# Reordering the second products of a two-stage mixture-of-experts kernel, with five smaller moves around them

## The chip, the cores and the metric

One NeuronCore of one Trainium2 chip runs the whole program. The metric is device time in microseconds (us) from one launch to its end; a kernel's time is the median of its runs. The names used here: PE is TensorE, DVE is VectorE, ACT is ScalarE, POOL is GpSimd, SP is SyncE, whose only work here is to issue DMAs.

## What is computed

The reference is three layers in a row, all in float32.

```python
def reference(**kwargs):
    attn_out = _attn_ref(q, k, v)                 # 2 x 8 heads, 768 rows, 64 wide, windowed
    x = attn_out as (1536 tokens, 512)
    x = _moe_ref(x, w_gate, w1, w2)               # each token through ONE of 8 experts (argmax)
    return _moe2_ref(x, w_gate, w1, w2)           # every token through ALL 8 experts

def _moe2_ref(x, w_gate, w1, w2):
    logits = x @ w_gate
    P = np.exp(logits - logits.max())
    for _ in range(8):                            # the "mixing"
        P /= P.sum(1, keepdims=True) + 1e-09
        P /= P.sum(0, keepdims=True) + 1e-09
        P *= N / E
    for e in range(E):
        h = np.maximum(x @ w1[e], 0.0)            # 1536 x 512 times 512 x 1024
        out += P[:, e:e + 1] * (h @ w2[e])        # 1536 x 1024 times 1024 x 512
    return out
```

## The kernel before

**First mixture (lines 775 to 1000).** Tokens are sorted by expert into blocks of 256 rows; seven blocks run here. `layer1` makes the hidden rows, `layer2` multiplies them with `w2`: two row groups `s` of 128 rows, eight chunks `fc` of the hidden size, three matmuls for each pair (the values are kept as a high and a low part). Before the change both groups go through `fc` 0 to 3 together, then group 0 through 4 to 7, then group 1. When a group is done its sum of squares is taken (L931), it is scaled (L936) and scattered to rows of `yd` in DRAM by an indirect DMA from POOL's queue (L937). Between the groups the next block's rows are turned on PE (`turn_rows`, L892, L897, L898). `step()` takes the next item of a list of weight loads and splits for the next block. Up to here a planner with a cost model decides each engine's order from when it thinks operands are ready; the program's order only breaks ties.

**Second mixture (lines 1000 to 1500).** Every product of four 2x2 quarters is done with seven products and additions (Strassen-Winograd form), so operands need sums. `tokens(j)` fetches a pair of 128-token tiles from `yd` (one of each half of the tokens), turns them on PE (L1066), copies them out (L1070), and makes the high and low part of seven operands: `part1` to `part5`, with the additions `sums12` and `sums34`. Its `logits` multiplies with the gate and, for each second pair, writes the operands to DRAM.

From L1477 on the order of each engine is written out by hand as a loop over ticks. Each tick issues what `plan` holds for it, then one first product (`first`, six matmuls: one of seven operands `i`, for one of four column chunks `fc`), and on every other tick one second product (`second`, twelve matmuls). An expert `e` takes 84 ticks; s below is its first tick, and the second products run 38 ticks behind. What follows a first product is spread over the next ticks (`operands2`): rounding the three raw parts (L1290, L1293), four additions on DVE (L1296 to L1299), rounding the four sums on ACT and DVE (L1302, L1305). They recur every seven ticks; "phase" below is the tick modulo 7, and the four additions are at phase 0, L1302 at phase 3 ahead of the eviction of first product 3 (called C1 below, L1257), L1305 at phase 4.

**The seven second products** of a group of 128 rows accumulate in two PSUM tiles. `gx` takes products 0, 3, 5, 6 one upon the other, each evicted before the next may be added: x0, x3, x5, x6. `ga` has two halves: y1, and z2 with z4 added to it. Evictions go to `acc`: products 2 and 4 by DVE (L1366), the others by ACT into `y` tiles (L1374), which two accumulating DMAs from POOL add to `acc` (L1368, L1376). For expert 0 nothing is scaled: products 4 and 5 are added by DVE (L1358), the rest are copied by ACT. For the last expert all are evicted by DVE and sent out by SP. After the last first product, second products are issued one per tick.

**Weights and mixing.** A `Piece` is a quarter of an expert's `w1` or `w2`: loaded, squared on ACT (`measure`, L690), its scale found through a PE matmul (`measured` L694 on DVE, then `rate` L699), sums made by POOL (L707, L711), and both parts written (L715 on ACT, L720 on DVE). The last quarter of `w2` takes over a buffer of the expert before, so `second` itself issues its splits at products 4 and 6 of the last row group. `mixing` is the eight rounds of normalising, 12 x 8 values per partition, each round two steps between ticks 66 and 115, where expert 0's second products and expert 1's weight splits run too.

## Time and profile before

| | before |
|---|---|
| median of 3 runs | 1277.93 us (1274.8 to 1278.49) |
| the profiled execution | 1278.5 us, of it a span of 1276.7 us |
| mean granted clock of PE | 0.979 of 2.4 GHz |
| PE busy | 1196.2 us (94%) |
| DVE, ACT, POOL busy | 999.5 (78%), 849.2 (67%), 364.1 us (29%) |
| chain that ended last, by engine | PE 66%, DVE 18%, DMA 7%, issue 5%, ACT 4% |
| attention and sorting | 0 to about 128 us |
| first mixture | about 128 to 320 us |
| second mixture | about 320 us to the end |

The span runs from the first to the last instruction; the rest of an execution's time, 1.8 us here, lies around it. PE's busy time is modelled and covers the overlap of matmuls, so PE's waits and the starts of its products say more than its share. A product's matmuls follow each other faster than the length that a row gives for one of them: 12 of them start within 1.31 us, while one is shown 0.27 us long. A wait is counted from the shown end, so a stall costs PE 0.16 us (0.27 less 1.31/12) more than its wait.

### The profile page before, as it was taken

Reading aid. Unit: us, or ns where it says so; the run is one execution under the profiler, and the core shown is the slowest. Engines: PE = TensorE matmul, PEld = TensorE weight load, DVE = VectorE, ACT = ScalarE, POOL = GpSimd, SP = SyncE. Lnnn points to the kernel's source line nnn. Section 1 sums busy time; section 2 is a strip of 40 time slices with the busy share of each in tenths; the row PEclk is TensorE's granted clock in tenths of the full one; section 3 lists DMA queues with packets and bytes.
Section 4 is the critical chain, followed back from the end, with each engine's and each line's share of the span. In section 5 each row is a group of like instructions: output and inputs, shape, how many; then the busy total and the mean of one; then the engine's idle time right before and its main releaser. Section 6 shows DMA issues by size and latency. Waiting matters only on the chain.

```text
span 1276.7 us, 27622 instructions
## 1 busy us (share of the span) xinstructions
PE 1196.2 (94%) x10551; PEld 1054.5 (83%) x10551; DVE 999.5 (78%) x1823; ACT 849.2 (67%) x1599; POOL 364.1 (29%) x412
## 2 busy tenths in 40 slices
PE   5898999999789889999999999999999999999997
PEld 5776879888578778888888888888888888888886
DVE  6695678975498899887888788788868878886674
ACT  5585578765476757776876776677668767775541
POOL 4351212102013142333434243243413334331000
PEclk8799999999799999999999999999999999999999
DMA  9954888764334414635444564445555534553201
GB/s 199 202 96 146 260 258 267 254 205 155 126 105 137 117 59 127 154 92 136 112 113 127 127 162 104 100 116 133 125 132 142 123 95 122 141 125 79 80 34 50
DMA packets 177597, 173.59 MB, mean 136 GB/s; under 512 B 32864, under 2 KB 149472, under 8 KB 177072
## 3 DMA queue, kind: packets, MB, share of 16 engines
q1 hardware_dynamic: 163888, 143.75, 39.1%
q0 software_dynamic: 13568, 27.99, 11.3%
q8 instruction: 85, 1.39, 0.5%
q14 instruction: 56, 0.46, 0.1%
HBM read 136.10 MB, written 15.53 MB: 119 GB/s over the span
## 4 chain that ended last, share of the span: by engine, by line
PE 66%; DVE 18%; DMA 7%; issue 5%; ACT 4%; SPq 1%; POOL 0%; DVEq 0%; ACTq 0%; POOLq 0%
PE gx L1336 16%; PE fx L1250 15%; PE ga L1336 12%; PE fa L1250 11%; DMA raw<-in_moe_w 3%; PE ph L814 3%; PE py L833 3%; DVE w1l L720 2%; DVE hl L1293 2%; DVE c L1260 1%; DVE wl L781 1%; DVE c L1297 1%; DVE c L1298 1%; DMA xl<-xold 1%; DVE c L1299 1%
## 5 line engine op out<-in xcount | busy, mean ns | idle before, releaser
L1336 PEld LDWEIGHTS <-hh 128*128 128x128 f16 x2688 | 263.2, 98 | 55.0 <-issue 24.4
L1250 PEld LDWEIGHTS <-w1h 128*128 128x128 f16 x2688 | 260.4, 99 | 49.4 <-issue 16.4
L1336 PE MATMUL gx<-w2h,hh 128*128 128x256 f16 x768 | 209.5, 273 | 7.7 <-DVE acc L1358 4.9
L1250 PE MATMUL fx<-xh,w1h 128*128 128x256 f16 x736 | 201.7, 274 | 9.2 <-ACT c L1257 4.8
L1336 PE MATMUL gx<-w2h,hl 128*128 128x256 f16 x768 | 209.5, 273 | 0.0
L1336 PE MATMUL gx<-w2l,hh 128*128 128x256 f16 x768 | 209.5, 273 | 0.0
L1250 PE MATMUL fx<-xl,w1h 128*128 128x256 f16 x736 | 201.6, 274 | 1.7 <-POOL xl L1076 1.0
L1250 PE MATMUL fx<-xh,w1l 128*128 128x256 f16 x736 | 201.8, 274 | 0.0
L1305 DVE TENSOR_TENSOR hl<-c,hh 128x1024 f16<-128x1024 f32 x96 | 120.5, 1255 | 84.1 <-ACT hh L1302 83.9
L707 POOL TENSOR_TENSOR raw<-raw 128x256 f32<-128x256 f32 x168 | 158.8, 960 | 55.9 <-ACT raw L690 46.9
L1336 PE MATMUL ga<-w2h,hh 128*128 128x256 f16 x576 | 157.0, 273 | 14.2 <-DVE acc L1366 14.2
L1257 ACT ACTIVATE c<-fx,kap 128x256 f32<-128x256 f32 x288 | 131.8, 473 | 54.5 <-PE fx L1250 53.0
L1336 PE MATMUL ga<-w2h,hl 128*128 128x256 f16 x576 | 157.1, 273 | 0.0
L1336 PE MATMUL ga<-w2l,hh 128*128 128x256 f16 x576 | 157.0, 273 | 0.0
L1250 PE MATMUL fa<-xh,w1l 128*128 128x256 f16 x552 | 151.6, 275 | 0.0
L1250 PE MATMUL fa<-xh,w1h 128*128 128x256 f16 x552 | 151.6, 275 | 0.0
L1250 PE MATMUL fa<-xl,w1h 128*128 128x256 f16 x552 | 151.6, 275 | 0.0
L1250 PEld LDWEIGHTS <-w1l 128*128 128x128 f16 x1344 | 132.2, 98 | 18.1 <-issue 1.9
L1336 PEld LDWEIGHTS <-hl 128*128 128x128 f16 x1344 | 131.5, 98 | 15.2
L1302 ACT CAST hh<-c 128x1024 f16<-128x1024 f32 x96 | 99.9, 1040 | 51.4 <-DVE c L1299 51.2
L1374 ACT ACTIVATE y<-gx,pws 128x256 f32<-128x256 f32 x144 | 68.1, 473 | 95.3 <-PE gx L1336 82.4
L711 POOL TENSOR_TENSOR raw<-raw 128x256 f32<-128x256 f32 x56 | 58.6, 1047 | 222.5 <-issue 155.1
(261 smaller groups left out, 2629.7 us busy)
## 6 DMA issues: line engine op xcount, KB each, us to landing
raw<-in_moe_w SPq DMA_DIRECT2D x64, 512.0 KB
raw<-in_moe_w SPq DMA_DIRECT2D x228, 128.0 KB
xh<-xohd SPq DMA_DIRECT2D x147, 128.0 KB
xl<-xold SPq DMA_DIRECT2D x147, 128.0 KB
acc<-y POOLq DMA_DIRECT2D x72, 256.0 KB, 4.3
raw<-in_moe_w SPq DMA_DIRECT2D x38, 256.0 KB
vt<-in_v SPq DMA_DIRECT2D x16, 240.0 KB
raw<-yd SPq DMA_DIRECT2D x12, 260.0 KB
```

Source lines behind the costliest of these rows:

```text
L707: eng.tensor_tensor(out=r[to], in0=r[x], in1=r[y], op=ALU.add if sign > 0 else ALU.subtract)
L711: eng.tensor_tensor(out=self.raw[:, 2], in0=self.raw[:, 2], in1=self.raw[:, 5 if self.second else 4], op=ALU.add)
L720: nc.vector.scalar_tensor_tensor(out=lo[:, w], in0=self.raw[:, s], scalar=wsc[self.x][:, self.i : self.i + 1], in1=hi[:, w], op0=ALU.mult, ...
L814: nc.tensor.matmul(ph, a, c[:, kc], start=kc == 0 and m == 0, stop=kc == KC - 1 and m == 2)
L833: nc.tensor.matmul(pys[s], a, c, start=fc == 0 and m == 0, stop=fc == FC - 1 and m == 2)
L1250: nc.tensor.matmul(p, l[:, a, kc * P : (kc + 1) * P], r[:, j, kc], start=new and kc == 0 and m == 0, stop=kc == K2 - 1 and m == 2, skip_gr ...
L1257: nc.scalar.activation(c[:, q], p, f, scale=k_)
L1293: nc.vector.scalar_tensor_tensor(out=h[1][:, :3], in0=raw, scalar=0.0, in1=h[0][:, :3], op0=ALU.max, op1=ALU.subtract)
L1302: nc.scalar.copy(h[0][:, 3:], c)
L1305: nc.vector.tensor_tensor(out=h[1][:, 3:], in0=c, in1=h[0][:, 3:], op=ALU.subtract)
L1336: nc.tensor.matmul(p, l, r, start=new and f == 0 and m == 0, stop=f == F2 - 1 and m == 2, skip_group_check=True)
L1374: nc.scalar.activation(gs["s"][:, d], p, AF.Copy, scale=w)
```

## The change

Six things are done:

1. `layer2`: both row groups go together through `fc` 0 and 1 only; then group 0 through 2 to 7, two steps, group 1 through 2 to 7.
2. The first two token pairs load, turn and split their first halves before their second halves.
3. The gate products of all pairs (`LOGITS`) come one or two ticks later; of expert 1's pieces four `rate` matmuls come two or three ticks later, and three of their squares move by one tick.
4. The mixing's two scalings per round go from DVE to POOL, each round gets a third step, and the constant NT/E moves into the column sum's scaling.
5. The seven second products run in the order x0, y1, x3, z2, x5, z4, x6 (before: x0, y1, z2, x3, z4, x5, x6). Each row half gets a `y` tile of its own. For expert 0, product 5 is copied by ACT into a `y` tile and added to `acc` by a DMA from POOL ("staged"), instead of being added by DVE.
6. The last quarter's splits are put into the plan at ticks of their own, 1 to 7 ticks after product 4, instead of at products 4 and 6. Its buffer is held four ticks longer, by which one other piece of each expert from the third on loads and splits three ticks later.

```diff
@@ layer2 @@
-        half = FC // 2
-        for fc in range(half):
+        for fc in range(2):
             for s in range(ns):
                 product(s, fc)
-            if fc % 2:
+        step()
+        step()
+        for s in range(ns):
+            for fc in range(2, FC):
+                product(s, fc)
+            if s == 0:
                 step()
                 step()
-        for s in range(ns):
-            for fc in range(half, FC):
-                product(s, fc)
             yield s, pys[s]
...
@@ tokens @@
-        def load():
+        def load(halves=(0, 1)):
...
-            for half in range(2):
+            for half in halves:
...
@@ mixing @@
-            nc.vector.tensor_tensor(out=pw, in0=pw, in1=r.unsqueeze(2).to_broadcast(sh), op=ALU.mult)
+            nc.gpsimd.tensor_tensor(out=pw, in0=pw, in1=r.unsqueeze(2).to_broadcast(sh), op=ALU.mult)
+
+        def turn2():
             cs.append(g2.tile([P, E], F32, tag="c", name="c"))
...
-            nc.vector.tensor_scalar(c, pc, 1e-9, None, op0=ALU.add)
+            nc.vector.tensor_scalar(c, pc, 1e-9, float(E / NT), op0=ALU.add, op1=ALU.mult)
             nc.vector.reciprocal(c, c)
-            nc.vector.scalar_tensor_tensor(
-                out=pw, in0=pw, scalar=float(NT / E), in1=c.unsqueeze(1).to_broadcast(sh), op0=ALU.mult, op1=ALU.mult
-            )
+            nc.gpsimd.tensor_tensor(out=pw, in0=pw, in1=c.unsqueeze(1).to_broadcast(sh), op=ALU.mult)
...
@@ second @@
-    SECOND = (
-        (H11, V11, "x", True),
-        (H12, V21, "y", True),
-        (R1, V1, "z", False),
-        (R2, V2, "x", False),
-        (R4, V22, "z", False),
-        (R3, V3, "x", False),
-        (H22, V4, "x", False),
-    )
+    SECOND = {
+        0: (H11, V11, "x", True),
+        1: (H12, V21, "y", True),
+        3: (R2, V2, "x", False),
+        2: (R1, V1, "z", False),
+        5: (R3, V3, "x", False),
+        4: (R4, V22, "z", False),
+        6: (H22, V4, "x", False),
+    }
...
             if i == 4:
-                last[e + 1].raw_hi()
-                last[e + 1].raw_lo()
-                last[e + 1].sum4()
-            elif i == 6:
-                last[e + 1].sum_hi()
-                last[e + 1].sum_lo()
+                p4 = last[e + 1]
+                for d, f in zip((0, 1, 2, 5, 6), (p4.raw_hi, p4.raw_lo, p4.sum4, p4.sum_hi, p4.sum_lo)):
+                    at(clock[0] + 1 + d, f)
...
-            if i in (4, 5):
+            if i == 4:
                 nc.vector.tensor_tensor(out=to, in0=p, in1=to, op=ALU.add)
+            elif i == 5:
+                y = yp.tile([P, DM], F32, tag="y", name="y")
+                nc.scalar.copy(y[:, hi], p)
+                nc.gpsimd.dma_start(out=to, in_=y[:, hi], accum_op=ALU.add)
...
-            gs["s"] = yp.tile([P, DM], F32, tag="y", name="y")
-        nc.scalar.activation(gs["s"][:, d], p, AF.Copy, scale=w)
+            gs[h] = yp.tile([P, DM], F32, tag="y", name="y")
+        nc.scalar.activation(gs[h][:, d], p, AF.Copy, scale=w)
...
@@ the plan @@
-    for j in (0, 1):
-        pairs[j][LOAD]()
+    for half in range(2):
+        for j in (0, 1):
+            pairs[j][LOAD]((half,))
...
-    for step in (TURN, P1_, S12, P2_):
+    for j in (0, 1):
+        pairs[j][TURN]((0,))
+    for j in (0, 1):
+        pairs[j][P1_]()
+    for j in (0, 1):
+        pairs[j][TURN]((1,))
+    for step in (S12, P2_):
...
-        for step, tick in ((P3_, 1), (S34, 3), (P4_, 4), (P5_, 5), (LOGITS, 13 + j)):
+        for step, tick in ((P3_, 1), (S34, 3), (P4_, 4), (P5_, 5), (LOGITS, 14 + 2 * j)):
...
-    turns = [66 + 6 * i + t for i in range(8) for t in (0, 4)]
+    turns = [66 + 6 * i + t for i in range(8) for t in (0, 2, 4)]
...
-            for p, i, load, square, rate in ((p1[3], 1, -23, -19, -16), (p2[3], 0, -23, -16, -12), (p2[1], 1, -18, -13, -10), (p2[2], 0, -15, -9, -6)):
+            for p, i, load, square, rate in ((p1[3], 1, -23, -18, -13), (p2[3], 0, -23, -16, -10), (p2[1], 1, -17, -12, -7), (p2[2], 0, -15, -10, -4)):
...
-                end = s + 37
-                assert load < s + 20, (p.e, p.second, p.j, load - s)
+                end = s + 41
+                assert load < s + 18, (p.e, p.second, p.j, load - s)
```

## Rows read from the trace of the kernel before

**Rows 1.** Waits of PE: who, for whom: us in total, times, longest us.

```profile
PE ga L1336 <- DVE acc L1366: 14.2, 8, 2.2
...
PE gx L1336 <- DVE acc L1358: 4.9, 4, 2.8
...
PE pz L699 <- DVE sqb L694: 3.1, 2, 2.1
...
PE gx L1336 <- DVE acc L1366: 2.8, 3, 1.6
```

**Rows 2.** Busy us by engine, 423.6 to 507.6 us: PE, PEld, DVE, ACT, POOL.

```profile
423.60:507.60 84.00, 75.10 (x689) 66.43 (x688) 78.24 (x170) 57.27 (x99) 22.91 (x25) 1.00 0.34 101
```

**Rows 3.** The chain: start us, us, what: prices of PE's pieces, and the tail.

```profile
253.27 2.75 PE py L833 x12
...
1236.80 0.66 PE fa L1250 x6
...
1247.72 1.48 PE ga L1336 x12
...
1260.15 1.32 PE gx L1336 x12
...
1261.50 0.49 DVE acc L1366
```

**Rows 4.** Timeline of ACT and POOL, end of the first mixture.

```profile
313.33 0.69 ACT L936 ACTIVATE yb<-py,sc 128x512 f32<-128x512 f32 x1 [0.62 <-DVE yb L633]
...
310.94 1.04 POOL L937 DMA_INDIRECT yd<-yb,row_i  x1 [14.85 <-ACT yb L936]
316.69 1.01 POOL L937 DMA_INDIRECT yd<-yb,row_i  x1 [4.71 <-DMA yd<-yb,row_i]
```

**Rows 5.** Timeline of PE, start of the second mixture.

```profile
325.85 1.94 PE L1066 MATMUL pt<-ident,raw 128*128 128x128 f32 x8 [0.88 <-issue]
329.50 0.37 PE L1250 MATMUL fx<-xh,w1h 128*128 128x256 f16 x1 [1.71 <-ACT xh L1075]
...
338.18 0.27 PE L1250 MATMUL fx<-xl,w1h 128*128 128x256 f16 x1 [0.97 <-POOL xl L1076]
```

**Rows 6.** Timeline of PE and DVE around the fourth pair's gate product.

```profile
365.60 0.18 PE L1120 MATMUL pz<-wgs,bl 128*128 128x8 f16 x1 [2.00 <-DVE bl L1110]
...
370.54 0.75 DVE L1260 SCALAR_TENSOR_TENSOR c<-fa,kap,c 128x512 f32<-128x512 f32 x1 [0.94 <-PE fa L1250]
```

**Rows 7.** Groups by line: busy us, mean ns of one, idle before them.

```profile
L720 DVE SCALAR_TENSOR_TENSOR w2l<-raw,wsc,w2h 128x768 f16<-128x768 f32 (+1 forms) x64 | 75.0, 1184 | 12.0 <-ACT w2h L715 10.3 <-DMA xh<-xohd 1.7
...
L431 POOL TENSOR_TENSOR ee<-ee,sm 128x512 f32<-128x512 f32 x24 | 24.9, 1042 | 29.6 <-DVE sm L430 14.1 <-DVE rank L375 3.7 <-ACT et L439 2.8
...
L1191 DVE SCALAR_TENSOR_TENSOR pw<-pw,c 128x96 f32<-128x96 f32 x8 | 2.9, 364 | 0.3
...
L1358 DVE TENSOR_TENSOR acc<-gx,acc 128x256 f32<-128x256 f32 x6 | 2.5, 412 | 0.0
L1181 DVE TENSOR_TENSOR pw<-pw,r 128x96 f32<-128x96 f32 x8 | 2.4, 300 | 0.3
```

**Rows 8.** Timeline around the start of expert 3: PE, DVE, ACT, POOL.

```profile
684.92 0.27 PE L1336 MATMUL ga<-w2h,hh 128*128 128x256 f16 x1 [2.18 <-DVE acc L1366]
...
683.65 0.83 DVE L1299 TENSOR_TENSOR c<-c 128x256 f32<-128x256 f32 x1
684.40 0.47 DVE L1366 SCALAR_TENSOR_TENSOR acc<-ga,pws,acc 128x256 f32<-128x256 f32 x1
...
691.88 0.42 DVE L1299 TENSOR_TENSOR c<-c 128x256 f32<-128x256 f32 x1
...
685.46 0.83 ACT L1257 ACTIVATE c<-fx,kap 128x256 f32<-128x256 f32 x2
...
682.43 2.63 POOL L707 TENSOR_TENSOR raw<-raw 128x256 f32<-128x256 f32 x3
```

More of the change, by code (lines that the diff above doesn't have):

```diff
@@ L1060, in load, with turn @@
                 nc.sync.dma_start(out=xw[half], in_=yd[t * P : (t + 1) * P])
-        def turn():
-            for half in range(2):
+        def turn(halves=(0, 1)):
+            for half in halves:
                 p = (pf_ if j == 1 else pg).tile([P, KC, P], F32, tag="x", name="pt")
@@ L1180, in turn1, with turn3 @@
             nc.vector.reciprocal(r, r)
-            nc.vector.tensor_tensor(out=pw, in0=pw, in1=r.unsqueeze(2).to_broadcast(sh), op=ALU.mult)
+            nc.gpsimd.tensor_tensor(out=pw, in0=pw, in1=r.unsqueeze(2).to_broadcast(sh), op=ALU.mult)
+        def turn2():
             cs.append(g2.tile([P, E], F32, tag="c", name="c"))
             nc.vector.tensor_reduce(out=cs[-1], in_=pw.rearrange("p t e -> p e t"), axis=AX.X, op=ALU.add)
-        def turn2():
+        def turn3():
             c = cs[-1]
@@ L1198, in end @@
             weigh(0)
-        return [gates1, gates2, start1, start2, start3] + [turn1, turn2] * 8 + [end]
+        return [gates1, gates2, start1, start2, start3] + [turn1, turn2, turn3] * 8 + [end]
     def weigh(e):
@@ L1367, in second @@
             if i == 4 and e < E - 1:
-                nc.gpsimd.dma_start(out=to, in_=gs["s"], accum_op=ALU.add)
+                nc.gpsimd.dma_start(out=to, in_=gs[0], accum_op=ALU.add)
             if e == E - 1 and i in (4, 5, 6):
@@ L1372, in second @@
         if i in (0, 5):
-            gs["s"] = yp.tile([P, DM], F32, tag="y", name="y")
-        nc.scalar.activation(gs["s"][:, d], p, AF.Copy, scale=w)
+            gs[h] = yp.tile([P, DM], F32, tag="y", name="y")
+        nc.scalar.activation(gs[h][:, d], p, AF.Copy, scale=w)
         if i == 6:
-            nc.gpsimd.dma_start(out=acc[:, t], in_=gs["s"], accum_op=ALU.add)
+            nc.gpsimd.dma_start(out=acc[:, t], in_=gs[1], accum_op=ALU.add)
     plan = {}
+    clock = [0]
     def at(tick, f):
@@ L1394, in body @@
     for j in (0, 1):
-        for step, tick in ((P3_, 1), (S34, 3), (P4_, 4), (P5_, 5), (LOGITS, 13 + j)):
+        for step, tick in ((P3_, 1), (S34, 3), (P4_, 4), (P5_, 5), (LOGITS, 14 + 2 * j)):
             at(tick, pairs[j][step])
     for j, load, turn in ((2, 6, 11), (3, 7, 20), (4, 20, 32), (5, 29, 42)):
-        for step, tick in ((LOAD, load), (TURN, turn), (S12, turn + 2), (P1_, turn + 3), (S34, turn + 4), (P2_, turn + 5), (P3_, turn + 6), (P4_, turn + 7), (P5_, turn + 8), (LOGITS, turn + 11)):
+        for step, tick in ((LOAD, load), (TURN, turn), (S12, turn + 2), (P1_, turn + 3), (S34, turn + 4), (P2_, turn + 5), (P3_, turn + 6), (P4_, turn + 7), (P5_, turn + 8), (LOGITS, turn + 13)):
             at(tick, pairs[j][step])
-    turns = [66 + 6 * i + t for i in range(8) for t in (0, 4)]
+    turns = [66 + 6 * i + t for i in range(8) for t in (0, 2, 4)]
     for tick, f in zip([55, 58, 62] + turns + [115], mix[2:]):
@@ L1468, in body @@
         for k in range(CHUNKS):
-            rest += [(e, k, s, i) for s in range(2) for i in range(7)]
+            rest += [(e, k, s, i) for s in range(2) for i in SECOND]
     LAG = 6
@@ L1475, in body @@
         while rest or plan:
+            clock[0] = tick
             for f in plan.pop(tick, ()):
```

## The prediction

> **What bounds the kernel now.** I read the chain that ended last first: two thirds of it are PE, so a microsecond counts if PE loses it by standing still. So next the list of what PE waited for, which names the places [rows 1], then busy time by engine in the stretches where these waits lie, then the timelines around single waits. Three things are to be seen. First, PE loses 14.2 us because the second half of `ga` is still being evicted when z4 wants it; seven of these eight waits lie where an expert's first products begin, the eighth in the tail [rows 1]. Second, from 424 to 508 us, while the mixing runs, DVE is busy 78.24 of 84.00 us [rows 2]: a queue that full runs behind PE, and there PE waits for expert 0's additions (4.9 us with one earlier wait) and for the cast ahead of a `rate` matmul (3.1 us) [rows 1]. Third, in the tail, where products stand back to back, each x6 waits for x5's eviction (2.8 us in three waits) [rows 1].
>
> **The prices.** A `py` matmul takes 0.23 us (2.75 / 12), a first product 0.66, a second 1.31 [rows 3]. The sum is made against the profiled execution, 1278.5 us; the median is 0.6 lower, and I take that off at the end.
>
> **The change part by part.**
>
> *Layer 2.* Group 0 of a block now ends six `py` matmuls sooner, 6 x 0.23 = 1.4 us. At the end of the last block this is on the path: group 0's scatter leaves POOL at 310.94, and group 1's, ready at 313.33 + 0.69 = 314.02, leaves only at 316.69, since it waited for the first one's landing [rows 4]. Both move up by 1.4, and with them the token loads behind; the room for it is 316.69 - 314.02 = 2.67. Gain 1.4. In the six other blocks one weight split waits six matmuls longer for its buffer, and the planner may order ACT anew; I see no wait at those seams that is sure to go or come, and bound each way by the one shift, 1.4; I take nothing.
>
> *First tokens.* The second pair's first half lands fourth part sooner: it is now the second load, not the third. PE began that pair at 325.85 and the first product only at 329.50, when the casts, queued on ACT behind all four copies, were done [rows 5]. Now two copies come ahead of the first casts, so the first product could start up to 329.50 - 325.85 = 3.6 us sooner. But its third operand still needs the halves that land last, with the same copies, additions and splits behind them, and the wait at 338.18 for POOL's split hangs on that [rows 5]. I take 2.0, between nothing and 3.6.
>
> *Gate products later.* PE stood 2.00 us for the fourth pair's `bl`; afterwards DVE stood idle 0.94 us waiting for PE [rows 6], so the loss was not given back. Two ticks are 1.31 us of first products at least, so the wait goes mostly, but the additions behind `bl` on DVE then bind ACT's next evictions. I take 1.4, between nothing and 2.0 + 0.16. The DMAs that these steps issue pass no other load on SP's queue.
>
> *Mixing to POOL, staged addition, `rate` later: 424 to 508 us.* DVE loses 8 x (0.300 + 0.364) = 5.3 us of scalings and 6 x 0.412 = 2.5 us of x5 additions, two of these outside the stretch [rows 7]. What the copies and DMAs of the staged addition add lies on ACT and POOL, busy 57.27 and 22.91 us of the 84 [rows 2]; if their cover were gone each copy would cost about what the addition did, 0.41. No row has POOL's 128x96 product. Its bounds are 0.30 us, what DVE took, and 1.04 us, POOL's like product on 512 columns [rows 7]; I take 0.5, the size being nearer to the first. Behind each waits DVE's next reduction of that round, two ticks later, and behind that all of DVE's evictions; two ticks hold 2.6 us of PE's work (one second product and two firsts), so 0.5 is covered unless POOL has three sums in hand. The products also slow DVE: an addition of 0.42 us took 0.83 beside POOL's sums [rows 8]. I charge 1.5 us for sixteen of them (0 to 16 x 0.5 = 8). DVE then needs 78.2 - 5.3 - 1.6 + 1.5 = 72.8 of 84, no longer more than PE. The Trainium skill (SBUF — State Buffer, Who interferes with whom) has the stronger rule that a VectorE instruction with two SBUF inputs and a GpSimd one that reads SBUF exclude each other, the loser standing for the whole instruction; the row agrees in kind, and by the rule the charge would be the upper 8, more than the 5.3 saved. The `rate` matmuls now have two or three ticks after the cast, where they had one or two. So of 4.9 + 3.1 = 8.0 us of waits I take 7.0 back; the bounds are nothing and 8.0 plus 7 x 0.16.
>
> *The new order at an expert's start.* z2 and z4 stay two products apart, but each stands one place later, that is two ticks later against the four additions of phase 0. The case of expert 3: PE was free at 684.92 - 2.18 - 0.16 = 682.58 and waited for z2's eviction, which stood on DVE behind additions stretched by POOL's three sums [rows 8]. Now x5 runs there (1.31), then one first product (0.66), so that PE gets to the next one at 684.55. That one adds onto C1, whose eviction is queued on ACT behind L1302, which waits for the same four additions: it starts at 685.46 and takes about 0.45, so PE starts at 685.95 [rows 8]. The wait shrinks from 2.34 to 1.40, by 0.94. x3 now follows x0 after one product instead of two; ACT has the four ticks between, 5.2 us at least, for x0's eviction, so this costs nothing unless ACT falls that far behind. Six such boundaries and one small wait of about 0.4: 6 x 0.94 + 0.4 = 6.0; the bounds are nothing and the whole 14.2 - 1.0 plus 7 x 0.16 = 14.3.
>
> *The last quarter's splits.* They were ready six ticks before x3 needs their sums; now `sum_lo` is issued at s + 41 and the product that reads it comes at s + 42. By hand it is just in time if DVE is not behind. I charge 1.5 us over seven experts, between nothing and 7 x 1.18 [rows 7]. `sum4` moves behind both accumulating DMAs on POOL, with three ticks to spare before ACT needs it. The later POOL DMA of row half 0 holds its `y` tile two ticks longer; ACT may wait for it, and has a third of its time free. The three ticks by which one piece loads later cost nothing: its splits fall into ticks with no others. Nothing is charged for these.
>
> *The tail.* x6 now has z4 between itself and x5: 1.32 against an eviction of 0.49 [rows 3]. All three waits go: 2.8 + 3 x 0.16 = 3.3. The wait before 1247.72 [rows 3] stays: x5 now waits there for x3's eviction, behind the same DVE work. The last two output DMAs come closer together, for which I take off 0.2: 3.1, between 2.5 and 3.3.
>
> **The sum.** 1.4 + 2.0 + 1.4 + 7.0 + 6.0 - 1.5 + 3.1 = 19.4 us. 1278.5 - 19.4 - 0.6 = 1258.5; I say 1258.
>
> **The rivals.**
>
> *The boundaries go whole* (and the mixing stretch too). For it: DVE may arrive less late, being relieved of x5's place. Against it: the chain through C1 in rows 8 hangs on the same additions. It gives 8.3 + 1.3 more: 1249.
>
> *POOL's products hold DVE up*, by the rule above or because DVE's next reduction waits for them. For it: the 0.83 against 0.42 in rows 8. Against it: 96 columns are short, and POOL is busy a quarter of the stretch. The mixing stretch then gains nothing, or loses 3: 1265 to 1268.
>
> *The waits only change their names.* PE waits for DVE at all these places, and where DVE or ACT is the bound a reorder moves the wait to the next product. Then only layer 2's end, the first tokens and the tail remain, 6.5 us, or the tail alone, if the planner puts the first two back: 1272 to 1275.
>
> *The last quarter comes too late* (slower). If at s + 41 DVE stands more than the tick behind, three splits (this piece's raw and sums, the next piece's raw) of 1.18 us each [rows 7] lie between PE and x3: 7 x 3 x 1.18 = 24.8 us instead of 1.5, so 1258 + 23.3 = 1281. It decides from a wait of (19.4 + 1.5) / 7 = 3.0 us for each expert.
>
> **How the numbers follow.** Forecast (1251 to 1264) 0.55; boundaries whole 0.15; POOL holds DVE up 0.15; names only 0.10; last quarter late 0.05. The range reaches down to 1246, as the first rival with a good seam in the first mixture, and up to 1271, over the third one; what it leaves out is the fifth case, most of the fourth, and some of the second. A measurement of this kernel tells about 0.3% from no change, 3.8 us, so faster is below 1274.1. The first three cases are, and half of the fourth: 0.90; same is the other half, 0.05; slower 0.05.
>
> **What would show it.** Right: group 1's scatter still leaves 5.75 us after group 0's, both 1.4 sooner, at 309.5 and 315.3; the first `fx` starts before 328; between 424 and 508 no wait for L1358 longer than 1 us, and DVE busy near 73 us instead of 78 for the same ticks; at each expert's start one wait of `fx` for ACT near 1.4 us, none of `ga` near 2; in the tail no wait of `gx` over 0.2. Wrong: DVE's additions at 0.8 us throughout ticks 66 to 112, waits of DVE for POOL's `pw`, or a wait of PE for L720 at the third second product of each expert.

## The result: slower by 0.6 to 0.75%

The changed kernel took 1287.65 us (median of 8 runs, 1282.49 to 1290.07) where the kernel before took 1276.61 (8 runs, 1273.45 to 1283.32): a ratio of 1.0075, 95% interval 1.005 to 1.010. Measured again beside other kernels, it was 1.0061 (1.0044 to 1.0079). The forecast was 1258, faster. The profiled execution of the changed kernel took 1283.4 us, with a span of 1281.5.

Lines move by one to four: the first products are now on L1251, the second on L1337, the four additions on L1297 to L1300, ScalarE's cast behind them on L1303, the evictions on L1368 (VectorE) and L1376 (ScalarE), the accumulating transfers on L1370 (product 4) and L1378 (product 6).

What PE waited for in the changed kernel (engine, line, releaser: us in total, times, longest), over the whole span:

```profile
PE fx L1251 <- ACT c L1258: 31.6, 19, 2.8
...
PE gx L1337 <- DVE w2l L720: 3.0, 6, 0.6
PE pz L699 <- DVE gsc L627: 2.4, 1, 2.4
PE pz L1191 <- DVE c L1186: 2.4, 2, 1.4
...
PE gx L1337 <- DVE acc L1368: 1.0, 1, 1.0
```

The waits of [rows 1] are gone: those of `ga`, those for the addition of expert 0, those of x6 in the tail (the 1.0 that is left is the wait that the prediction kept, ahead of x5). But first products now wait 31.6 us for ScalarE, where they waited 4.8 us in six waits before. The groups by line of VectorE, changed kernel (busy us, mean ns of one):

```profile
L1298 DVE TENSOR_TENSOR c<-c 128x256 f32<-128x256 f32 x96 | 62.6, 652 | 3.3
L1299 DVE TENSOR_TENSOR c<-c 128x256 f32<-128x256 f32 x96 | 57.0, 593 | 3.3
L1297 DVE SCALAR_TENSOR_TENSOR c<-c 128x256 f32<-128x256 f32 x96 | 56.4, 588 | 0.0
...
L1300 DVE TENSOR_TENSOR c<-c 128x256 f32<-128x256 f32 x96 | 51.1, 533 | 3.3
...
L1204 DVE TENSOR_SCALAR pws<-pw,winv 128x12 f32<-128x12 f32 x8 | 14.3, 1782 | 0.0
```

Nothing was added to these instructions, yet the four additions take 227.1 us (208.0 in the kernel before, 209.3 in the first experiment below, which has the old order), and the product that scales the gates, twelve elements in each partition, takes 1782 ns (280 and 275 there). And ScalarE's cast behind the additions stood idle for them, in the group's own line, 115.9 us (51.2 in the kernel before). Changed kernel, then the kernel before:

```profile
L1303 ACT CAST hh<-c 128x1024 f16<-128x1024 f32 x96 | 100.2, 1043 | 116.0 <-DVE c L1300 115.9
```

```profile
L1302 ACT CAST hh<-c 128x1024 f16<-128x1024 f32 x96 | 99.9, 1040 | 51.4 <-DVE c L1299 51.2
```

**Where the time went.** I set the two traces side by side by the start of VectorE's first addition (one every seven ticks), and summed by stretch: an expert's stretch runs from the addition at its first tick s to the one at the next expert's first tick. "Each" is the mean over experts 2 to 6; the tail runs from the addition at tick 672, the last but one, to the end.

| us | to expert 1 | expert 1 | experts 2 to 6, each | expert 7 | tail |
|---|---|---|---|---|---|
| before | 448.6 | 119.8 | 113.31 | 108.2 | 33.59 |
| changed | 438.6 | 126.0 | 115.86 | 107.3 | 30.32 |

The early parts were 10 us ahead in this pair of executions, and the tail brought 3.27, against a forecast of 3.1. But expert 1 lost 6.2 and each of experts 2 to 6 lost 2.55, where the forecast had a gain of some 0.9 (less the charge for the splits).

**One expert's start.** Timelines of the changed kernel ahead of expert 3 (start us, us, engine, line, what [idle before <-releaser]): VectorE, GpSimd, ScalarE, PE.

```profile
666.55 0.74 DVE L1368 SCALAR_TENSOR_TENSOR acc<-ga,pws,acc 128x512 f32<-128x512 f32 x1
667.21 1.01 DVE L720 SCALAR_TENSOR_TENSOR w1l<-raw,wsc,w1h 128x768 f16<-128x768 f32 x1
...
668.20 3.11 DVE L1297 SCALAR_TENSOR_TENSOR c<-c 128x256 f32<-128x256 f32 x1
671.35 1.34 DVE L1298 TENSOR_TENSOR c<-c 128x256 f32<-128x256 f32 x1
672.73 0.43 DVE L1299 TENSOR_TENSOR c<-c 128x256 f32<-128x256 f32 x1
673.19 0.42 DVE L1300 TENSOR_TENSOR c<-c 128x256 f32<-128x256 f32 x1
...
667.83 0.87 POOL L1370 DMA_DIRECT2D acc<-y  x1 [8.41 <-ACT y L1376]
668.42 1.04 POOL L707 TENSOR_TENSOR raw<-raw 128x256 f32<-128x256 f32 x1
669.10 1.04 POOL L711 TENSOR_TENSOR raw<-raw 128x256 f32<-128x256 f32 x1
669.78 1.03 POOL L707 TENSOR_TENSOR raw<-raw 128x256 f32<-128x256 f32 x1
670.45 1.20 POOL L1378 DMA_DIRECT2D acc<-y  x1
671.03 1.37 POOL L707 TENSOR_TENSOR raw<-raw 128x256 f32<-128x256 f32 x1
...
673.64 1.04 ACT L1303 CAST hh<-c 128x1024 f16<-128x1024 f32 x1 [5.30 <-DVE c L1300]
674.60 0.47 ACT L1258 ACTIVATE c<-fx,kap 128x256 f32<-128x256 f32 x1
...
675.12 0.27 PE L1251 MATMUL fx<-xh,w1h 128*128 128x256 f16 x1 [2.68 <-ACT c L1258]
```

Read it from below. PE waits 2.68 us for an eviction on ScalarE; that stands behind the cast, which waited 5.30 us for the four additions of tick s - 7; the first of these took 3.11 us, while GpSimd ran three additions of weight quarters and a transfer back to back. GpSimd had all these in hand because its queue had stood 8.41 us behind product 4's transfer, which can go only when product 4 has been evicted; and that eviction (666.55) now stands in VectorE's queue just ahead of the additions, with a split and a cast of 0.15 us between. In the kernel before the same four, VectorE's timeline, then GpSimd's from the second of its additions beside them:

```profile
670.73 0.41 DVE L1296 SCALAR_TENSOR_TENSOR c<-c 128x256 f32<-128x256 f32 x1
671.18 0.83 DVE L1297 TENSOR_TENSOR c<-c 128x256 f32<-128x256 f32 x1
672.04 0.83 DVE L1298 TENSOR_TENSOR c<-c 128x256 f32<-128x256 f32 x1
672.91 1.54 DVE L1299 TENSOR_TENSOR c<-c 128x256 f32<-128x256 f32 x1
...
671.69 0.91 POOL L707 TENSOR_TENSOR raw<-raw 128x256 f32<-128x256 f32 x1
672.54 0.87 POOL L1376 DMA_DIRECT2D acc<-y  x1
673.12 1.04 POOL L707 TENSOR_TENSOR raw<-raw 128x256 f32<-128x256 f32 x1
```

The wait can be taken apart, counting from the start of the first addition. Before, PE came to this product 4.81 us after it and ran it at 5.22; the profile shows 0.25 us idle there. In the changed kernel PE comes at 4.07, since the additions start later against PE (product 4's eviction, 0.66 us of VectorE's queue, is now ahead of them), and the eviction lets it go at 6.91. So of the 2.68 - 0.25 = 2.43 us, 0.74 come from the later start, and 6.91 - 5.22 = 1.69 from the longer additions.

### The profile page after: what moved, and what is told of

The parts are those of the page before. It is cut to its first block, busy times and chain, and to the rows that moved or that the text cites. A ratio compares the mean times of both kernels' runs of the same rounds, so it can differ in the third digit from the quotient of the medians.

```text
span 1281.5 us, 27664 instructions
## 1 busy us (share of the span) xinstructions
PE 1194.4 (93%) x10551; PEld 1050.3 (82%) x10551; DVE 1024.4 (80%) x1801; ACT 848.9 (66%) x1605; POOL 368.1 (29%) x434
## 4 chain that ended last, share of the span: by engine, by line
PE 55%; DVE 20%; ACT 9%; DMA 8%; issue 7%; SPq 1%; POOL 0%; DVEq 0%; ACTq 0%; POOLq 0%
PE gx L1337 13%; PE fx L1251 13%; PE fa L1251 10%; PE ga L1337 10%; DMA raw<-in_moe_w 4%; PE ph L814 3%; PE py L833 2%; DVE c L1297 2%; DVE w2l L720 2%; ACT raw L690 2%; DVE c L1298 2%; DVE c L1261 2%; DVE w1l L720 2%; DVE c L1299 1%; DVE hl L1294 1%
## 5 line engine op out<-in xcount | busy, mean ns | idle before, releaser
L1251 PEld LDWEIGHTS <-w1h 128*128 128x128 f16 x2688 | 259.5, 98 | 75.6 <-issue 42.8
L1337 PEld LDWEIGHTS <-hh 128*128 128x128 f16 x2688 | 264.0, 98 | 32.5 <-issue 1.2
L1251 PE MATMUL fx<-xh,w1h 128*128 128x256 f16 x736 | 201.1, 273 | 31.5 <-ACT c L1258 29.7
L1337 PE MATMUL gx<-w2l,hh 128*128 128x256 f16 x768 | 210.4, 274 | 3.0 <-DVE w2l L720 3.0
L1337 PE MATMUL gx<-w2h,hh 128*128 128x256 f16 x768 | 210.5, 274 | 1.0 <-DVE acc L1368 1.0
L1337 PE MATMUL gx<-w2h,hl 128*128 128x256 f16 x768 | 210.3, 274 | 0.0
L1251 PE MATMUL fx<-xl,w1h 128*128 128x256 f16 x736 | 201.3, 274 | 1.0 <-POOL xl L1077 1.0
L1251 PE MATMUL fx<-xh,w1l 128*128 128x256 f16 x736 | 201.4, 274 | 0.0
L707 POOL TENSOR_TENSOR raw<-raw 128x256 f32<-128x256 f32 x168 | 162.3, 975 | 66.0 <-ACT raw L690 41.5
L1303 ACT CAST hh<-c 128x1024 f16<-128x1024 f32 x96 | 100.2, 1043 | 116.0 <-DVE c L1300 115.9
L1306 DVE TENSOR_TENSOR hl<-c,hh 128x1024 f16<-128x1024 f32 x96 | 123.7, 1288 | 42.8 <-ACT hh L1303 42.7
L1337 PE MATMUL ga<-w2h,hh 128*128 128x256 f16 x576 | 157.2, 273 | 0.0
L1337 PE MATMUL ga<-w2l,hh 128*128 128x256 f16 x576 | 157.1, 273 | 0.0
L1337 PE MATMUL ga<-w2h,hl 128*128 128x256 f16 x576 | 157.0, 273 | 0.0
L1251 PE MATMUL fa<-xh,w1h 128*128 128x256 f16 x552 | 150.8, 273 | 0.9 <-ACT xh L1076 0.9
L1251 PE MATMUL fa<-xl,w1h 128*128 128x256 f16 x552 | 150.8, 273 | 0.5 <-DVE xl L1077 0.5
L1251 PE MATMUL fa<-xh,w1l 128*128 128x256 f16 x552 | 150.7, 273 | 0.0
L1337 PEld LDWEIGHTS <-hl 128*128 128x128 f16 x1344 | 132.0, 98 | 19.8 <-issue 4.1
L1251 PEld LDWEIGHTS <-w1l 128*128 128x128 f16 x1344 | 132.0, 98 | 17.9 <-issue 1.6
L1294 DVE SCALAR_TENSOR_TENSOR hl<-c,hh 128x768 f16<-128x768 f32 x96 | 94.8, 988 | 19.7 <-ACT hh L1291 19.4
L1376 ACT ACTIVATE y<-gx,pws 128x256 f32<-128x256 f32 x144 | 68.1, 473 | 62.3 <-PE gx L1337 34.4
```

What stands on the lines that cost most here:

```text
L707: eng.tensor_tensor(out=r[to], in0=r[x], in1=r[y], op=ALU.add if sign > 0 else ALU.subtract)
L1251: nc.tensor.matmul(p, l[:, a, kc * P : (kc + 1) * P], r[:, j, kc], start=new and kc == 0 and m == 0, stop=kc == K2 - 1 and m == 2, skip_gr ...
L1294: nc.vector.scalar_tensor_tensor(out=h[1][:, :3], in0=raw, scalar=0.0, in1=h[0][:, :3], op0=ALU.max, op1=ALU.subtract)
L1303: nc.scalar.copy(h[0][:, 3:], c)
L1306: nc.vector.tensor_tensor(out=h[1][:, 3:], in0=c, in1=h[0][:, 3:], op=ALU.subtract)
L1337: nc.tensor.matmul(p, l, r, start=new and f == 0 and m == 0, stop=f == F2 - 1 and m == 2, skip_group_check=True)
```

## The experiments

Two theories (others stand with the expectations where they are needed). **C**, collision: GpSimd's additions of weight quarters, bunched behind product 4's late transfer, run beside VectorE's additions and hold them up. **W**: the new places of the evictions in the queues of VectorE and ScalarE cost the time by themselves. Beside these stood the question which part of the change loses and which gains. All ratios are to the kernel before on the same chip; the last three columns are those of the table above, each from one traced execution. The expectations count a wait with the 0.16 us that a stall costs beyond it (2.98, 1.44, 2.34), the text and the fences as the profile shows it (2.82, 1.28, 2.18).

| | ratio (95%) | median us | expert 1 | 2 to 6, each | tail |
|---|---|---|---|---|---|
| 1 old order | 0.9986 (0.9975 to 0.9996) | 1273.1 | 120.0 | 113.29 | 33.59 |
| 2 new order alone | 1.0122 (1.0098 to 1.0146) | 1291.1 | 125.9 | 115.80 | 30.32 |
| 3 old places of the splits | 1.0018 (1.0005 to 1.0031) | 1277.1 | 123.5 | 114.89 | 30.32 |
| 4 new order in expert 7 only | 0.9940 (0.9919 to 0.9961) | 1268.7 | 121.6 | 113.29 | 30.33 |
| 5 changed, no GpSimd additions | 0.9843 (0.9798 to 0.9887) | 1256.0 | 121.2 | 110.91 | 30.32 |
| 6 old order, no GpSimd additions | 0.9806 (0.9771 to 0.9841) | 1250.1 | 114.0 | 110.24 | 33.59 |
| 7 gates' product on ScalarE | 1.0057 (1.0038 to 1.0076) | 1283.7 | 126.8 | 115.64 | 30.33 |
| 8 as 4, additions later | 0.9907 (0.9874 to 0.9940) | 1263.5 | 120.9 | 112.07 | 30.32 |
| 9 mixing's stretch alone | 1.0005 (0.9989 to 1.0020) | 1275.2 | 120.0 | 112.95 | 33.58 |
| 10 start alone | 0.9987 (0.9971 to 1.0002) | 1273.7 | 120.4 | 113.30 | 33.59 |
| 11 changed, additions later | 1.0004 (0.9988 to 1.0020) | 1275.3 | 124.2 | 114.64 | 30.32 |
| 12 changed, transfer later | 1.0159 (1.0131 to 1.0188) | 1295.4 | 123.4 | 118.21 | 30.32 |
| 13 as 5, in expert 1 too | 0.9812 (0.9795 to 0.9828) | 1252.5 | 118.8 | 111.09 | 30.33 |
| 14 changed, again | 1.0061 (1.0044 to 1.0079) | 1283.3 | 126.1 | 115.72 | 30.32 |
| 15 as 8, from expert 1 on | 0.9871 (0.9853 to 0.9889) | 1260.6 | 121.5 | 112.07 | 30.32 |

### 1 and 2: the order out, the order alone

```diff
-            rest += [(e, k, s, i) for s in range(2) for i in SECOND]
+            rest += [(e, k, s, i) for s in range(2) for i in sorted(SECOND)]
 (and the last quarter's splits back beside products 4 and 6)
```

> The changed kernel with the seven second products and the last quarter's splits back in the old order and ticks; everything else of the change stays. Theory O (the new order of the products loses what the early parts gained: in the changed kernel's trace the lead of 10.8 us at tick 133 is gone by tick 252 and each later expert gives up some 2.8 us): 1287.7 less 7 for expert 1 and 6 x 2.8 for experts 2 to 7, plus the 3.3 that the tail gained, so 1267, and faster than the kernel before by 0.6 to 1.0%. Rival M (the loss comes from mixing's products on GpSimd and from the later rates, whose effects last into expert 1 and beyond): at least 1280.

Experiment 2 is the kernel before with `SECOND`, the two staging tiles and the splits of the changed kernel, nothing else.

> The kernel before with nothing changed but the order of the second products and the last quarter's splits that go with it. Theory O: every expert from 1 on gives up about 2.8 us (some 19 in all), the tail gives 3.3 back: 1292. If the prediction was right about the order (6.0 gained at the expert starts, 3.1 in the tail, 1.5 lost to the splits): 1269. Rival M: between 1268 and 1275.

Theory O held in its direction: the order alone (with its splits and staging tiles) made the kernel before 1.2% slower, and from expert 1 on every stretch of it is that of the changed kernel. But without the order the rest of the change brings only 1.4 us, not the 11.8 of the prediction, so the first experiment ended 6 us above the 1267 that theory O gave it: that figure came off one pair of traces. The parts also do not add up: beside the new order the rest of the change is worth 6 to 8 us (1.0122 against 1.0075 and 1.0061), beside the old one 1.4 to 1.8. Why is not known; the intervals of the ratios are 1 to 3 us to either side. The two experiments also show where the tail's gain lies: 33.59 with the old order, 30.32 with the new.

### 3: the last quarter's splits

```diff
             if i == 4:
-                p4 = last[e + 1]
-                for d, f in zip((0, 1, 2, 5, 6), ...):
-                    at(clock[0] + 1 + d, f)
+                (raw_hi, raw_lo, sum4 here, sum_hi and sum_lo at i == 6)
```

> The changed kernel, its new order kept, but the last quarter's splits issued as in the kernel before: three beside product 4, two beside product 6. Since product 4 now runs sixth and product 6 seventh, the five steps fall on two neighbouring ticks. Theory H (the splits at ticks of their own, up to tick 13 of the expert, cause the loss): 1272 or less. Theory O without H (the loss is in the evictions and their queues): within 4 us of the changed kernel's 1287.7, at most 0.65 us per expert better (the wait on the splits at tick 6 of an expert).

Between the two: 5.5 to 7.3 us better than the changed kernel. The edit also gives the buffer back its four ticks. The waits for L720 (3.0 us in six) are gone, so are 2.3 us of each of VectorE's cycles from tick 35 to 42, and in expert 1 first products wait 3.4 us for ScalarE in four waits, not 5.2. What is left, 1.6 us per expert against the old order and 3.5 in expert 1, is the order's own, with the five steps of the splits on two neighbouring ticks.

### 4: the new order where it costs nothing

```diff
+            for i in (SECOND if e == E - 1 else sorted(SECOND))
```

> As the changed kernel with the old order and the old splits, but with the new order in the last expert alone. Theory O: the old order keeps the early parts' gain in experts 1 to 6, and the new order gives its tail: 3 us less than the kernel with the old order throughout, about 1264, if the last expert's own blocks, which have no accumulating DMA and no splits, do not lose what the others lose (some 2.8 us); if they do, the two cancel and it ends at the old order's time.

As theory O has it: 4.5 us under experiment 1 by the medians, 3.26 in the traces' tails. In the last expert no product is staged, and no splits or transfers wait.

### 5 and 6: GpSimd's additions left out

```diff
         def sums(...):
+            if self.e >= 2:
+                return
 (the same in sum4)
```

> The changed kernel with GpSimd's additions of weight quarters (lines 707 and 711) left out for experts 2 to 7, so their outputs are not the reference's; loads, splits, products, evictions and accumulating transfers stay. Theory C (the loss is a collision: product 4's transfer, later in GpSimd's queue, bunches these additions beside VectorE's four additions and its small product with the gates; VectorE waits for GpSimd's run): the waits of 2.98 and 1.44 us at each expert start and of 0.65 us at tick 42 go, and with them at least 4 us per expert: 1262 or less, and within 3 us of the same edit on the old order. Theory W (not the collision but the order of the evictions in the queues of VectorE and ScalarE): within 5 us of the changed kernel's 1287.7.

> The kernel with the old order (the first experiment) with the same additions of GpSimd left out. Theory C: the old order pays for the same collision too (four additions of VectorE in 3.7 us beside GpSimd's, against 1.7 alone), so the wait of 2.34 us at each expert start shrinks to 0.5 or less: 1273 less 6 x 2, so 1261 or less. Theory W: the wait stays at 2.3, the time within 4 us of 1273; the new order with the same edit ends at least 10 us later than this.

Theory C in the main: 2.2 to 2.3% of the time on the new order, 1.8% on the old, more than it asked for. This is what all of GpSimd's additions of experts 2 to 7 cost, not those at the expert starts alone. In the sixth, PE waits for nothing at all in experts 2 to 6; in the fifth the waits at the starts are 0.5 us or less. The four additions of the new order, ahead of expert 3:

```profile
662.69 0.41 DVE L1301 SCALAR_TENSOR_TENSOR c<-c 128x256 f32<-128x256 f32 x1
663.14 0.42 DVE L1302 TENSOR_TENSOR c<-c 128x256 f32<-128x256 f32 x1
663.60 0.42 DVE L1303 TENSOR_TENSOR c<-c 128x256 f32<-128x256 f32 x1
664.06 0.43 DVE L1304 TENSOR_TENSOR c<-c 128x256 f32<-128x256 f32 x1
...
662.31 0.86 POOL L1374 DMA_DIRECT2D acc<-y  x1 [17.18 <-ACT y L1380]
662.85 1.21 POOL L1382 DMA_DIRECT2D acc<-y  x1
```

GpSimd issues both transfers in these 1.8 us and the additions do not feel it: it is GpSimd's arithmetic that holds VectorE, not its transfers by themselves. But theory C had said that the two orders would end within 3 us of each other, and they lie 5.9 apart: 0.67 us for each of experts 2 to 6 and 7.2 in expert 1, whose own pieces kept their additions, less what the tail gives back. So W has a part too; experiment 13 asks how large.

### 7: the product of twelve gates

```diff
-        nc.vector.tensor_scalar(pws[:, :, e], pw[:, :, e], winv[e % 2], None, op0=ALU.mult)
+        nc.scalar.activation(pws[:, :, e], pw[:, :, e], AF.Copy, scale=winv[e % 2])
```

> The changed kernel with the product of gates and scale (line 1204, 12 elements per partition, 2.24 us in the changed kernel, 0.23 in the kernel before) moved from VectorE to ScalarE, at the same place of the order. Theory C: those 2.0 us of VectorE go and the cycle from tick 35 to 42 of each expert loses most of its 1.9 us: 1276 to 1282. Theory W: no change, within 3 us of 1287.7.

A miss: 1.0057 is not to be told from 1.0061 and 1.0075, and VectorE's cycle from tick 35 to 42 takes 11.12 us (11.20 in the changed kernel). The product is held up beside GpSimd's additions (2.6 us for 0.2), but that does not set the time there; the third experiment, in which this cycle is 2.3 us shorter, points to the splits.

### 8, 11 and 15: the additions at other ticks

```diff
-                at(load + 7 + i_, ...sums(i_))      -  at(begin + 2, p.sum4)
+                at(load + 10 + i_, ...sums(i_))     +  at(begin + 4, p.sum4)
 (for experts 2 to 7; in experiment 15 for expert 1 too)
```

> The fourth experiment's kernel (old order, new order in the last expert alone), with GpSimd's additions of weight quarters issued 3 ticks later and the fourth of each piece 2 ticks later, so that they fall behind VectorE's four additions and not beside them. Theory C: the wait of 2.34 us at each expert start falls below 1.3: 1268.7 less 6 us, so 1259 to 1265. Theory W: no gain, 1268 or more (or worse, if the splits now wait for the additions).

> The changed kernel with GpSimd's additions of weight quarters 3 ticks later and the fourth of each piece 2 ticks later, for experts 2 to 7: the edit of the eighth experiment, here on the new order. Theory C (collision): it is worth at least what it was worth on the old order (5 us there), and up to the 2.98 + 1.44 us of each expert start: 1266 to 1282. Theory W (eviction order): within 4 us of 1287.7.

> The eighth experiment's kernel with expert 1's additions of weight quarters moved later in the same way. Theory C: expert 1, with waits of 0.6 to 2.0 us in the old order, gains up to 2 us: 1261 to 1263. Without a collision there: 1263.5, as the eighth experiment.

Theory C in kind, smaller in size. On the old order the wait of 2.18 fell to 1.67 only (1.83 with the 0.16, where below 1.3 was expected), and each expert gained 1.2 us; on the new order the wait of 2.68 fell to 1.79 and the kernel gained 7 to 9 us by the ratios. The two engines' additions still meet, only less: at tick s GpSimd's fourth is released by a split that stands just ahead of VectorE's four. Experiment 15 took 1260.6 us, 1.3% under the kernel before, and beats both kernels; but from the eighth it is not to be told (0.9853 to 0.9889 against 0.9874 to 0.9940), and its trace shows expert 1 no shorter, so its own step is open.

### 12: product 4's transfer later

```diff
-                nc.gpsimd.dma_start(out=to, in_=gs[0], accum_op=ALU.add)
+                at(clock[0] + 3, lambda y=gs[0]: nc.gpsimd.dma_start(out=to, in_=y, accum_op=ALU.add))
```

> The changed kernel with only product 4's accumulating transfer issued three ticks later, behind product 6's, so that it no longer stands at the head of GpSimd's queue ahead of the additions of weight quarters. Theory H (it is this transfer, waiting for the late eviction of product 4, that bunches the additions): the four additions of VectorE at tick s-7 fall from 5.4 to 3.7 us or less, the wait of 2.98 to 1.4 or less: 1275 to 1280, if ScalarE doesn't wait for the staging tile. If the bunching comes from the fourth addition of each piece (line 711, which waits for VectorE's split) as much as from the transfer: within 4 us of 1287.7.

The mechanism was right, the time wrong by 15 us and more: the condition, that ScalarE should not wait for the staging tile, did not hold. VectorE, ahead of expert 5, ScalarE behind it, and PE:

```profile
904.10 0.41 DVE L1297 SCALAR_TENSOR_TENSOR c<-c 128x256 f32<-128x256 f32 x1
904.54 0.83 DVE L1298 TENSOR_TENSOR c<-c 128x256 f32<-128x256 f32 x1
905.41 0.83 DVE L1299 TENSOR_TENSOR c<-c 128x256 f32<-128x256 f32 x1
906.27 1.53 DVE L1300 TENSOR_TENSOR c<-c 128x256 f32<-128x256 f32 x1
...
910.86 0.47 ACT L1376 ACTIVATE y<-gx,pws 128x256 f32<-128x256 f32 x1 [1.60 <-DMA acc<-y]
...
911.75 0.27 PE L1251 MATMUL fx<-xh,w1h 128*128 128x256 f16 x1 [1.62 <-ACT c L1258]
```

The additions are back at 3.7 us and the wait of 2.68 to 2.83 is 1.1: it is this transfer, at the head of GpSimd's queue, that bunches. But the staging tile now comes free too late, ScalarE stands, and PE waits again 2.4 us on, for 1.62 to 1.79 us at all six starts: what the additions gave back is lost there. ScalarE's waits from 655 to 1130 us, this kernel and, for comparison, the changed one:

```profile
ACT y L1376 <- DMA acc<-y: 46.3, 23, 4.3
```

```profile
ACT y L1376 <- DMA acc<-y: 6.1, 7, 2.0
```

### 9 and 10: the early parts, each alone

Experiment 9 is the kernel before with mixing's products on GpSimd in three steps, the staged addition and the later rates; experiment 10 with the second layer's order, the tokens' first halves and the later gate products.

> The kernel before with the changes of the stretch from 424 to 508 us alone: mixing's two products on GpSimd with the column sums in a step of their own, the addition of the first expert's sixth product staged, the four rates of expert 1 later. The prediction's step gave this 7.0 us: 1269. Rival N (the waits change names: in the kernel with the old order the lost waits on line 1358 are followed by new ones on line 1186's column sums, 0.98 and 1.29 us, and on the scales, 2.1 us): a gain of 2 or less, 1272 to 1275.

> The kernel before with the changes of the start alone: the second layer of the first mixture ends its first rows sooner, the tokens' first halves are loaded and turned first, the gate products come later. The prediction's steps gave this 1.4 + 2.0 + 1.4 = 4.8 us: 1270. Rival N: the second layer gains nothing, since the first mixture took 172.8 us in the kernel before and 173.1 to 175.8 in the kernels with the new one; tokens and gate products gain 3.4: 1272 to 1273.

Rival N in both: 0.6 us lost (by the interval from 1.4 gained to 2.5 lost) and 1.7 gained (from 0.3 lost to 3.7); together about what experiment 1 shows. PE's waits from 395 to 510 us, the kernel before, then experiment 9:

```profile
PE gx L1336 <- DVE acc L1358: 4.1, 3, 2.8
PE pz L699 <- DVE sqb L694: 3.1, 2, 2.1
```

```profile
PE pz L699 <- DVE gsc L627: 1.9, 1, 1.9
PE pz L1190 <- DVE c L1185: 1.9, 2, 1.1
```

The two waits to be removed are gone, and others stand there: for the scale behind the `rate` matmul, and for the column sums that wait for GpSimd's product. All waits of the stretch together, 9.9 us, became 7.1. Why these 2.8 us don't appear in the time is not settled. Part may lie in the clock: PE's mean granted clock over the runs was 0.9809 of full speed in experiment 9 and 0.9823 in the kernel before, which is 1.8 us at full speed, but single runs spread from 0.976 to 0.988. For the start, traces and medians disagree: the stretch up to expert 1 took 438 to 443 us in the fourteen traced executions with the new start and 444 to 449 in the three with the old one, where all runs of the tenth experiment give the new start 1.7.

### 13 and 14: what collision doesn't explain, and the changed kernel again

Experiment 13 leaves GpSimd's additions out from expert 1 on; experiment 14 is the changed kernel.

> The changed kernel with GpSimd's additions of weight quarters left out for expert 1 as well (the fifth experiment left them out for experts 2 to 7), so the outputs are not the reference's. In the fifth and sixth experiments the new order still took 5.8 us more than the old one in expert 1 (119.50 us against 113.69), whose own pieces kept their additions. Theory C: those are the same collision: expert 1 falls to 115 or less, 1251 or less in all. Theory W: expert 1 stays above 118, the time at 1256.

> The changed kernel itself, beside the others on the same chip: 1.0075 of the kernel before, 1285 to 1288 if the kernel before takes 1275 to 1277; the waits of 2.9 to 3.0 us at the starts of experts 2 to 6 in the same places, each followed within 12 us by a wait of 1.4 us or by a stretch at the lower clock.

Expert 1 fell from 121.2 to 118.8 (the expectation measures this stretch from another point: its 119.50 is 121.2 here), and the time, 1252.5, lies between the two expectations; the old order has 114.0. PE's first products still wait 3.1 us there for ScalarE in four waits. So of the 6 to 7 us that the order costs in expert 1, at most about a third is collision with expert 1's own additions: the old order was not run without these, and might gain by it too. The rest I put down to the order (theory W), there where the mixing's end and expert 1's splits share the queues; that is argued, not shown. Experiment 14 ended some 2 us below what was expected. It has the waits, 2.67 to 2.81 us, at all six expert starts, in the same places. Those of experts 4 to 6 are followed by a wait of 1.28 some 8.7 us on; at those of experts 2, 3 and 7 PE's clock fell instead.

## Why the prediction was wrong, step by step

*Layer 2: 1.4 forecast, too little to be seen.* In the changed kernel the two scatters leave GpSimd at

```profile
308.35 1.04 POOL L938 DMA_INDIRECT yd<-yb,row_i  x1 [13.49 <-DVE xl L899]
313.06 1.01 POOL L938 DMA_INDIRECT yd<-yb,row_i  x1 [3.67 <-ACTq L983]
```

2.6 and 3.6 us sooner than in [rows 4], and 4.71 apart where 5.75 was forecast; but this execution's first mixture had started 3.0 us sooner. From its first matmul to its last the first mixture took 172.8, 173.1 and 174.3 us in the traces with the old second layer, 171.9 to 178.0 in those with the new.

*First tokens and gate products: 2.0 and 1.4 forecast.* The step itself worked: the first `fx` starts at 323.81, before 328, and 13.1 us after the last `py` (17.5 before): 4.4 sooner, over the bound of 3.6. It does so in every trace, 13.0 to 13.8 us with the new start against 17.5 to 18.4 with the old. But the tenth experiment, which has both and layer 2, gained 1.7 by the ratio. Other waits followed: 0.81 us of a gate product for the copy of the one before, and `fx` waits for ScalarE of 1.70, 1.42 and 0.53 us, against 1.38 and 0.57 in the kernel before. They do not explain it all, since in the traces the lead is still there at tick 42 (62 to 64 us after the last `py`, against 68 to 70); that stays open.

*Mixing, staged addition, rates: 7.0 forecast, none measured.* VectorE's load fell as I said it would, 74.34 of 84 us in the matching stretch against 78.24 in [rows 2]:

```profile
414.00:498.00 84.00, 78.59 (x708) 69.05 (x706) 74.34 (x157) 59.28 (x106) 36.84 (x44) 0.98 0.38 108
```

The failed step is the one from load to wait: I took back nearly all waits of the stretch because VectorE was no longer full on average. The waits changed names, the rival to which I gave 0.10; in part it is also the second rival, since the new waits for the column sums (1.9 us in experiment 9) stand behind GpSimd's products.

*The new order: 6.0 forecast, some 7 us lost by the medians with the splits in their old places* (experiment 3 against 1, 4.0, and the tail's 3.3 that is in it). I followed one queue, from z2's eviction to the C1 eviction for which the product at tick s + 6 waits, and that wait came out as forecast: 1.28 us shown, 1.44 with the 0.16, 1.40 said; and the waits of `ga` went. What the sum lacked is tick s - 7. There product 4's eviction now stands ahead of the four additions, and its transfer holds GpSimd's queue until just then. I had written of that transfer that it holds a tile longer, and charged nothing; the queue behind it I did not name. So at six starts, where PE had waited 0.53 and 0.25 us at two and not at all at the others, it now waits 2.68 to 2.83. A reading was off too: of the eight waits of `ga`, six lie at an expert's start, not seven; one, of 0.43 us, lies inside expert 1.

*GpSimd holding VectorE up.* I priced this collision, with the row of 0.83 against 0.42, but only in the mixing. It came at the expert starts, which this rival did not contain. The Trainium skill (SBUF — State Buffer, Who interferes with whom) says that a VectorE instruction with two SBUF inputs contends with a GpSimd instruction that reads SBUF, and that transfers do not slow compute engines; the fifth experiment's 0.42 us beside transfers and the changed kernel's 3.11 beside additions agree.

*The last quarter's splits: 1.5 forecast, 5.5 to 7.3 lost.* Of the kind forecast, a wait for L720 at tick s + 42, but 0.5 us at each of six experts and not the 3.5 of the rival, whose 1281 us came near the measured time by another way, which is luck. With the 0.16 each these waits make 4.0 us; 1.8 more are the longer waits for ScalarE in expert 1 (5.2 against 3.4). What may be left, up to 1.5, I could not place. The term was mis-sized.

*The tail: 3.1 forecast, 3.27 measured,* in every kernel with the new order.

Put together in medians: -1.4 (early parts, experiment 1), +4.0 for the order with its tail (3 against 1), +5.5 to 7.3 (splits): 8 to 10 us slower. The two measurements say 7.8 and 9.6. The steps go from kernel to kernel, so that they add up is no proof of any one. Of the 27 to 29 us between forecast and measurement the order is 13, the mixing 7 to 8, the splits 4 to 6, the start 3. In the first rival's sum the 1.3 for the mixing should have been 2.1 by its own bound (8.0 + 7 x 0.16 - 7.0), which makes 1248; nothing hangs on it.

## What to carry to other kernels

When an eviction moves, follow every queue that its result releases, the queue that issues its transfer above all: a transfer at the head of GpSimd's queue is a gate (8.41 us here), and whatever has piled up behind it runs when the gate opens. If that is arithmetic beside VectorE's, what matters is which VectorE instructions are next at that moment. And a wait that is relieved by a queue's mean load is relieved only if the next queue in line has been looked at in the same tick; a reorder that pays in one stage can be kept to that stage.

## What the runs showed of the hardware

A VectorE addition of 0.42 us alone took mostly 0.83 where it ran alternately with GpSimd's additions, but up to 3.11, through three additions and a transfer, in some places. What sets these apart is not which began first: at 668.20, and at 680.62 where the additions took 0.42 and then 0.83 three times, VectorE began 0.22 us before GpSimd's first addition by the profile's starts. It is a transfer that GpSimd issued directly ahead of its addition. In all seventeen traces, of 6528 of these additions 210 took more than 1.0 us, every one beside a GpSimd addition that follows directly on a transfer (311 have that); of the other 6217 none did. (The profile's spans on GpSimd are rough; this goes by its order of instructions.) Transfers without additions behind them slowed nothing (839 additions, 0.43 us at most). The product of the gates shows the same: 0.23 us alone, and in the changed kernel, VectorE and GpSimd,

```profile
728.82 2.64 DVE L1204 TENSOR_SCALAR pws<-pw,winv 128x12 f32<-128x12 f32 x1
...
728.44 0.87 POOL L1378 DMA_DIRECT2D acc<-y  x1 [1.76 <-ACT y L1376]
729.02 1.72 POOL L711 TENSOR_TENSOR raw<-raw 128x256 f32<-128x256 f32 x2
```

In the kernel before GpSimd's addition began beside it nearly as soon (0.16 us after it, 0.20 here), but with no transfer ahead, and it took 0.23. Why a transfer ahead does this no run shows.

PE's clock, window by window (us; busy of PE, PEld, DVE, ACT, POOL; granted clock), after the wait of 2.68 at expert 3's start in the changed kernel:

```profile
676.30:679.60 3.30, 3.30 (x18) 2.36 (x16) 3.27 (x7) 2.51 (x5) 0.00 (x0) 0.50 0.28 86
679.60:683.00 3.40, 3.40 (x33) 3.02 (x32) 3.30 (x6) 1.41 (x3) 2.08 (x3) 0.99 0.01 2
```

The clock fell to 0.50 of full speed, 1.2 of 2.4 GHz, for 3.4 us, some 16 matmuls at twice their time: 1.7 us lost. From 345 us to the last product, every such stretch in the seventeen traces began between 0.8 us before the end of a PE wait of 1.4 to 2.8 us and 1.7 us after it, but not every such wait has one. From the second mixture on the kernel before shows four, the old order three, experiment 3 seven, and experiment 6, which has no waits there, none in experts 2 to 7. They differ between executions of one kernel, and they hide a later wait: at each of thirty expert starts, in five traces with the new order and GpSimd's additions in their old places (the changed kernel twice, experiments 2, 3 and 7), either the clock fell or the wait of 1.28 followed, never both.
